# One normalisation for the nine softmax sums of a pair of heads, in the first batch

## The chip, the cores and the metric

The kernel runs on one core of one Trainium2 chip. The metric is the device time of one execution in microseconds, the median of several runs; lower is better. The core has a tensor engine for matrix products (PE, with its weight loads shown apart as PEld), a vector engine (DVE), a scalar engine (ACT), GpSimd (POOL), and a queue for transfers (SP). Each engine works through its own instructions in the order in which the program has them; engines wait for one another by semaphores.

## The reference

Three stages stand one behind the other; the change is in the first, in its first batch.

```python
# q, k, v: (4, 8, 576, 64); blocks of 64; a query sees its own block and those before it
scores = np.matmul(q, k.transpose(0, 1, 3, 2)) / np.sqrt(64)
scores = np.where(block_i >= block_j, scores, -1e9)
attn = np.exp(scores - np.max(scores, axis=-1, keepdims=True))
attn = attn / (np.sum(attn, axis=-1, keepdims=True) + 1e-09)
x = np.matmul(attn, v)                     # then laid out as 2304 tokens of 512
...
x = np.maximum(np.maximum(x @ w1, x @ w2), x @ w3) @ w_out          # 512 -> 768 -> 512
...
for e in range(4):                          # 512 -> 1024 -> 512 for each expert
    out += p[:, e:e + 1] * (np.maximum(x @ w1[e], 0.0) @ w2[e])
```

## The kernel before, in words

**The stages.** The attention is computed batch by batch, eight heads a batch, two heads (a pair) at a time. The first feed-forward stage (moe1, L549) of a batch is put between the attention of the next batch, in small steps. The experts come last and are the larger part of the time; they are almost nothing but matrix products. The weights of moe1 are converted during the first batches (class Convert, L417: two steps on ACT, L452 and L454, then POOL L459, DVE L461 and L462, POOL L466, ACT L85 and DVE L475).

**Scores of a head.** 576 queries are four blocks of 128 rows and one of 64. The last 64 rows of both heads of a pair share a fifth block, p4. scores(g, grp) (L163) computes head g in two groups: group 0 holds the blocks 0, 2 and 3, group 1 the block 1, and for the odd head of a pair the shared block as well. Each block is a product in PSUM (L190, L195), a row minimum on DVE (L208) and an exponential on ACT (L215), which also writes the row sum into one column of sm. So a pair has nine columns of sums: four for each head and one for the shared block.

**Normalising.** scores leaves a function normalise (L221) behind, which is called once the next step has been written (stage, L599). It adds 1e-9 to the sums of its group (DVE L223) and takes the reciprocal (DVE L224). In batches 1 to 3 POOL then multiplies each block by its reciprocals (L236). In batch 0 (g < H) only the shared block p4 is multiplied so. The other blocks stay as they are; POOL copies their reciprocals, each one 64 times side by side, into rb (L232), a part of the large tile arena that is free at that time. For each pair these are four copies, of 192 or of 64 elements a partition.

**Behind it.** turn_probs (L259) transposes the probabilities on PE (L274) into PSUM tiles tt, and DVE or ACT copies them to eh (L299; the shared block by L283). values32 (L311) multiplies them by v on PE (L320, L328, L332), and ACT copies the result to xf (L339 to L346). weigh (L349) transposes rb into a PSUM tile rt (L355), and DVE multiplies xf by it (L358). moe1_inputs (L537) splits xf into two parts (L546, L547).

**Buffers.** The score tiles of group 0, tt and rt all come from one pool of four PSUM banks, the x pool; the tile of the odd head's group 1, which holds the shared block, comes from a pool of one tile of its own, c. There are two tiles p4, one for each of two pairs in flight, and three tiles sm for the sums, one a head.

**What sets the order.** The loop over heads (L621) writes the steps of a head in the order of a list, todo; the code that it writes is then ordered for each engine by the framework's planner, on a timeline that it works out while the kernel is built (`schedule_with_timeline_sim=True`). So an engine's order in the trace is not always that of the source: work of the conversion stands between that of the heads, and the group of a head that has a buffer free can come ahead of its other group.

Of the kernel before, what the change touches and what calls it, by code (L numbers as in the profile page):

```python
# [18 lines left out]
P = 128  # L19
# [5 lines left out]
def program(tc, q, k, v, w123, w_out, probs, e_w1, e_w2, out):  # L25
    nc = tc.nc

    B, H, D, S = q.shape[0], 2 * q.shape[1], q.shape[2] // 2, q.shape[4]
# [5 lines left out]
    NPAIR = H // 2  # L34
# [22 lines left out]
    arena = big.tile([P, KD * NT], F32, name="arena")  # L57
# [24 lines left out]
    pairs, heads, later, made = {}, {}, [], {}  # L82
# [80 lines left out]
    def scores(g, grp):  # L163
        pair, h = pairs[g // 2], g % 2
        if grp == 0:
            heads[g] = dict(
                p=[None] * 4,
                mn=ap_.tile([P, 5], F32, name="mn", tag="mn", bufs=3),
                sm=ap_.tile([P, 5, 2], F32, name="sm", tag="sm", bufs=3),
            )  # L170
        mn, sm, pt = heads[g]["mn"], heads[g]["sm"][:, :, 0], heads[g]["p"]
        masked = g < 2 * H
        c0 = 3 * grp
        sets = []
        for tag, cols, plan in GROUPS[1][h] if grp else GROUPS[0]:
            st = (ps_x if tag == "x" else ps_c).tile([P, cols], F32, name="st", tag=tag)
            sets.append((st, plan))
            for i, o, w in plan:

                if i == 4:  # L180
                    todo = [(QT + 64 * x, x) for x in range(2)]
                else:
                    todo = [(h * QT // 2 + P * i, h)]
                c = 0
                while c < w:
                    n = min(w - c, 512 - (o + c) % 512)
                    terms = [(part, q0, x) for q0, x in todo for part in ("q1", "q2")]
                    ends = masked and i < 4 and c + n == w
                    for m, (part, q0, x) in enumerate(terms):
                        nc.tensor.matmul(  # L190
                            out=st[:, o + c:o + c + n], lhsT=pair[part][:, q0:q0 + P],
                            rhs=pair["kk"][:, x, c:c + n], start=m == 0, stop=m == len(terms) - 1 and not ends,
                        )
                    if ends:
                        nc.tensor.matmul(  # L195
                            out=st[:, o + w - 64:o + w], lhsT=corner, rhs=corner[:, 0:64], start=False, stop=True
                        )
                    c += n
        c = c0
        done = []  # L200
        for st, plan in sets:
            for i, o, w in plan:
                if i < 4 and not masked:
                    nc.vector.memset(st[lo, o + w - 64:o + w], 1e30)
            mine = [(c + n, *x) for n, x in enumerate(plan)]
            c += len(plan)
            for col, i, o, w in mine:
                nc.vector.tensor_reduce(mn[:, col:col + 1], st[:, o:o + w], axis=AX.X, op=ALU.min)  # L208
            for col, i, o, w in mine:
                x = ap_.tile([P, w], F32, name=f"p{i}", tag=f"p{i}", bufs=2 if i == 4 else 3)  # L210
                if i == 4:
                    pair["p4"] = x
                else:
                    pt[i] = x
                nc.scalar.activation(  # L215
                    x, st[:, o:o + w], ACTF.Exp, bias=mn[:, col:col + 1], scale=-1.0,
                    accum_out=sm[:, col:col + 1],
                )
                done.append((col, x))

        def normalise():  # L221
            cs = slice(c0, c)
            nc.vector.tensor_scalar(sm[:, cs], sm[:, cs], 1e-9, None, op0=ALU.add)  # L223
            nc.vector.reciprocal(sm[:, cs], sm[:, cs])  # L224
            if g < H:

                if grp == 0 and h == 0:
                    o = 4 * (g // 2) * P
                    pair["rb"] = arena[:, o:o + 4 * P].rearrange("p (i h c) -> p i h c", i=4, h=2)
                rb = pair["rb"][:, 0:3, h] if grp == 0 else pair["rb"][:, 3:4, h]  # L230
                rs = sm[:, c0:c] if grp == 0 else sm[:, c - 1:c]
                nc.gpsimd.tensor_copy(rb, rs.unsqueeze(2).to_broadcast([P, c - c0 if grp == 0 else 1, 64]))  # L232
            for col, x in done:
                if g < H and x is not pair.get("p4"):
                    continue
                nc.gpsimd.tensor_scalar(x, x, sm[:, col:col + 1], 1.0, op0=ALU.mult, op1=ALU.mult)  # L236

        later.append(normalise)


# [372 lines left out]
    all_of(prep_pair(0))  # L613
    load_pair(2)
    stage(scores, 0, 0)
    stage(scores, 0, 1)
    stage(all_of, prep_pair(1))
    load_pair(3)
    stage(scores, 1, 0)
    stage(scores, 1, 1)  # L620
    for g in range(NG_):  # L621
# [15 lines left out]
        for n, st in enumerate(todo):  # L637
# [8 lines left out]
            at = (g + (n + 1) / len(todo)) / H  # L646
# [552 lines left out]
    def tile_in(pool, tag, shape, dt, bufs=1):  # L1199
        if early.get((pool, tag)):  # L1200
            return early[pool, tag].pop(0)
        return pool.tile(shape, dt, name=tag, tag=tag, bufs=bufs)
# [69 lines left out]
    for p in range(1, NPASS):  # L1272
        es = list(range(E))[::-1] if p % 2 else list(range(E))
        background = mix() if p < NPASS - 1 else iter(())
        for m, e in enumerate(es):
# [4 lines left out]
            for n, i in enumerate(order):  # L1280
                if n % 2 == 0:
                    h = parts[f"hq0{n // 2}"] if m % 2 == 0 else tile_in(p3, f"hq1{n // 2}", HQ, F32)
# [85 lines left out]
```

## Time and profile before

| | |
|---|---|
| median of 3 runs | 1252.12 us (1251.15 to 1253.44) |
| profiled execution | 1249.5 us |
| its span, first to last instruction | 1247.6 us |
| PE busy in the span | 1210.9 us |
| DVE busy in the span | 934.0 us |
| mean granted clock of PE, as a share | 0.997 |

The span is that of one execution under the profiler; the 1.9 us between it and the execution's own time lie around it. Batch 0's attention ends at about 88 us of the span.

### The profile page before, as it was taken

The page shows a single profiled execution, that of the slowest core. Times are in us where ns is not written, and L with a number is a line of the kernel's source. Part 1 is how long each engine was busy: PE and PEld are TensorE (multiplying, and loading weights), DVE is VectorE, ACT ScalarE, POOL GpSimd, SP SyncE. Part 2 cuts the span into 40 slices and gives each one's busy share as a digit, 9 for nine tenths or more (in the row PEclk, how much of TensorE's full clock was granted, in tenths as well). Part 3 has the DMA queues.
Part 4 walks back from the last instruction along what each step waited for, and adds up shares of the span by engine and source line. Part 5 has one row for each costly group of instructions (what it writes and reads, how often), then busy time and mean ns, then how long its engine had stood idle before and what let it go on. Part 6 is the DMA issues. An engine that isn't in the chain of part 4 may idle for free.

```text
span 1247.6 us, 19748 instructions
## 1 busy us (share of the span) xinstructions
PE 1210.9 (97%) x7433; PEld 1157.6 (93%) x7433; DVE 934.0 (75%) x1720; ACT 516.4 (41%) x1076; POOL 339.0 (27%) x428
## 2 busy tenths in 40 slices
PE   6889998999999999999999999999999999999998
PEld 5668997999999999989999998999999999999998
DVE  8979888666565634378888886758787788586896
ACT  7976767544544421234434441233232222322232
POOL 3648786454344212243333341000000000000000
PEclk9999999999999999999999999999999999999999
DMA  8745475545533488479888865778787887766754
GB/s 320 266 144 194 162 263 167 168 151 156 182 103 118 120 298 293 154 305 336 306 308 297 312 239 169 281 279 317 294 310 308 313 315 289 253 251 235 253 203 178
DMA packets 82644, 299.69 MB, mean 240 GB/s; under 512 B 8748, under 2 KB 18036, under 8 KB 69492
## 3 DMA queue, kind: packets, MB, share of 16 engines
q1 hardware_dynamic: 82548, 298.42, 67.2%
q8 instruction: 59, 0.97, 0.3%
q14 instruction: 37, 0.30, 0.1%
HBM read 215.26 MB, written 83.14 MB: 239 GB/s over the span
## 4 chain that ended last, share of the span: by engine, by line
PE 71%; DVE 13%; DMA 7%; ACT 4%; issue 3%; POOL 2%; SPq 0%; DVEq 0%; ACTq 0%; POOLq 0%
PE m L883 22%; PE m L528 19%; PE o L1042 17%; DMA t<-in_e_w 3%; PE st L190 3%; PE pv L382 2%; PE tt L274 2%; PE m L1042 2%; DMA part<-in_e_w 2%; DVE mn L208 2%; PE o L965 1%; PE o L968 1%; PE o L969 1%; PE pv L328 1%; DVE w L838 1%
## 5 line engine op out<-in xcount | busy, mean ns | idle before, releaser
L528 PE MATMUL m<-xh,wt 128*128 128x288 f32 x1120 | 238.8, 298 | 1.9 <-DVE mt L566 1.6
L883 PE MATMUL m<-t,w 128*128 128x384 f32 x1152 | 228.5, 336 | 0.0
L1042 PE MATMUL o<-hx,w 128*128 128x384 f32 x1176 | 225.8, 337 | 0.0
L1042 PEld LDWEIGHTS o<-hx,w 128*128 128x128 f32 x1176 | 207.9, 188 | 0.0
L883 PEld LDWEIGHTS m<-t,w 128*128 128x128 f32 x1152 | 203.3, 188 | 2.6 <-DVE tmp L903 0.4
L528 PEld LDWEIGHTS m<-xh,wt 128*128 128x128 f32 x1120 | 183.8, 188 | 2.8 <-DVE mt L566 2.0
L883 PE MATMUL m<-b,w 128*128 128x384 f32 x864 | 175.7, 337 | 2.9 <-ACT tmp L908 2.9
L528 PE MATMUL m<-xl,wt 128*128 128x288 f32 x560 | 165.2, 295 | 0.0
L883 PEld LDWEIGHTS m<-b,w 128*128 128x128 f32 x864 | 153.2, 188 | 6.0 <-ACT tmp L908 3.2
L528 PEld LDWEIGHTS m<-xl,wt 128*128 128x128 f32 x560 | 105.2, 188 | 0.3
L903 DVE TENSOR_TENSOR tmp<-m,tmp 128x384 f32<-128x384 f32 x144 | 77.8, 549 | 18.7 <-PE m L883 18.3
L236 POOL TENSOR_SCALAR p<-p,sm 128x128 f32<-128x128 f32 (+4 forms) x112 | 73.7, 674 | 46.5 <-DVE sm L224 17.5
L528 PE MATMUL m<-hh,wo 128*128 128x288 f32 x384 | 81.3, 299 | 2.7 <-ACT arena L577 1.3
L215 ACT ACTIVATE p<-st,mn 128x128 f32<-128x128 f32 (+3 forms) x144 | 78.4, 554 | 8.3 <-DVE mn L208 7.8
L1013 ACT CAST hx<-hq 128x768 fp32r<-128x768 f32 x49 | 40.5, 836 | 99.2 <-PE o L1042 76.1
L190 PE MATMUL st<-kk,q 128*128 128x128 f32 (+4 forms) x336 | 70.3, 339 | 7.5 <-ACT q L133 5.3
L965 PE MATMUL o<-w,hh 128*128 128x512 f32 x192 | 74.7, 391 | 0.8 <-ACT hh L943 0.5
L968 PE MATMUL o<-w,hh 128*128 128x512 f32 x192 | 74.7, 390 | 0.0
L969 PE MATMUL o<-w,hl 128*128 128x512 f32 x192 | 74.1, 390 | 0.0
L838 POOL TENSOR_TENSOR w<-part,w 128x512 fp32r<-128x512 f32 x32 | 48.8, 1547 | 88.7 <-ACT w L836 71.3
L566 DVE TENSOR_TENSOR mt<-m,mt 128x288 f32<-128x288 f32 x96 | 43.1, 452 | 39.1 <-PE m L528 38.6
L208 DVE TENSOR_REDUCE mn<-st 128x1 f32<-128x128 f32 (+3 forms) x144 | 66.4, 504 | 2.8 <-PE st L195 2.5
(173 smaller groups left out, 2182.0 us busy)
## 6 DMA issues: line engine op xcount, KB each, us to landing
w<-kb SPq DMA_DIRECT2D x55, 1024.0 KB, 5.5
w<-ka SPq DMA_DIRECT2D x30, 1792.0 KB, 7.5
ka<-w SPq DMA_DIRECT2D x16, 1792.0 KB, 6.7
wt<-held SPq DMA_DIRECT2D x54, 512.0 KB, 4.1
kb<-part SPq DMA_DIRECT2D x16, 1024.0 KB, 6.9
kb<-w SPq DMA_DIRECT2D x16, 768.0 KB, 5.2
arena<-in_w SPq DMA_DIRECT2D x18, 512.0 KB, 4.1
wo<-held SPq DMA_DIRECT2D x12, 768.0 KB, 4.5
```

What stands on the lines that cost most here:

```text
L190: nc.tensor.matmul(out=st[:, o + c:o + c + n], lhsT=pair[part][:, q0:q0 + P], rhs=pair["kk"][:, x, c:c + n], start=m == 0, stop=m == len(t ...
L208: nc.vector.tensor_reduce(mn[:, col:col + 1], st[:, o:o + w], axis=AX.X, op=ALU.min)
L215: nc.scalar.activation(x, st[:, o:o + w], ACTF.Exp, bias=mn[:, col:col + 1], scale=-1.0, accum_out=sm[:, col:col + 1],)
L236: nc.gpsimd.tensor_scalar(x, x, sm[:, col:col + 1], 1.0, op0=ALU.mult, op1=ALU.mult)
L528: nc.tensor.matmul(out=out_, lhsT=w, rhs=x, start=m == 0, stop=m == n - 1)
L838: eng.tensor_tensor(w[:, a:b, 1], raw[:, a:b], f(w[:, a:b, 0]), op=ALU.subtract)
L883: ins = nc.tensor.matmul(out=m, lhsT=a, rhs=b, start=start and n == 0, stop=stop and n == 3 * KH - 1, skip_group_check=True,)
L903: nc.vector.tensor_tensor(t, x, y, op=ALU.add)
L965: ins = nc.tensor.matmul(out=o, lhsT=hh[:, ts], rhs=wh, start=i == 0, stop=False)
L968: nc.tensor.matmul(out=o, lhsT=hh[:, ts], rhs=wl, start=False, stop=False)
L969: nc.tensor.matmul(out=o, lhsT=hl[:, ts], rhs=wh, start=False, stop=i == G - 1)
L1042: nc.tensor.matmul(out=o, lhsT=a, rhs=b, start=start and m == 0, stop=stop and m == 2, skip_group_check=True,)
```

## The change

In batch 0 the sums of both heads of a pair stand in one strip of 18 columns of the arena (every second one is used), behind the region of rb. The exponentials write them there in the order of the blocks 0, 1, 2, 3 of the one head, those of the other, and the shared block. normalise does nothing in three of the four groups of a pair; in the last one (odd head, group 1) it adds 1e-9 to all nine sums, takes one reciprocal of nine, and has POOL copy eight of them into rb in one instruction of 512 elements a partition. The multiplication of p4 by the ninth follows. Batches 1 to 3 are as before.

```diff
+            if g < H:
+                o = 4 * NPAIR * P + 18 * (g // 2)
+                heads[g]["sm"] = arena[:, o:o + 18].rearrange("p (c two) -> p c two", two=2)
...
+                at = col if g >= H else 8 if i == 4 else 4 * h + (0, 3, 1, 2)[i]
                 nc.scalar.activation(
                     x, st[:, o:o + w], ACTF.Exp, bias=mn[:, col:col + 1], scale=-1.0,
-                    accum_out=sm[:, col:col + 1],
+                    accum_out=sm[:, at:at + 1],
                 )
-                done.append((col, x))
+                done.append((at, x))
 
         def normalise():
-            cs = slice(c0, c)
+            if g < H and not (grp and h):
+                return
+            cs = slice(0, 9) if g < H else slice(c0, c)
             nc.vector.tensor_scalar(sm[:, cs], sm[:, cs], 1e-9, None, op0=ALU.add)
             nc.vector.reciprocal(sm[:, cs], sm[:, cs])
             if g < H:
 
-                if grp == 0 and h == 0:
-                    o = 4 * (g // 2) * P
-                    pair["rb"] = arena[:, o:o + 4 * P].rearrange("p (i h c) -> p i h c", i=4, h=2)
-                rb = pair["rb"][:, 0:3, h] if grp == 0 else pair["rb"][:, 3:4, h]
-                rs = sm[:, c0:c] if grp == 0 else sm[:, c - 1:c]
-                nc.gpsimd.tensor_copy(rb, rs.unsqueeze(2).to_broadcast([P, c - c0 if grp == 0 else 1, 64]))
+                o = 4 * (g // 2) * P
+                pair["rb"] = arena[:, o:o + 4 * P].rearrange("p (i h c) -> p i h c", i=4, h=2)
+                nc.gpsimd.tensor_copy(
+                    pair["rb"].rearrange("p i h c -> p h i c"),
+                    sm[:, 0:8].rearrange("p (h i) -> p h i", h=2).unsqueeze(3).to_broadcast([P, 2, 4, 64]),
+                )
```

## Rows read from the trace of the kernel before

**Rows 1.** The page's first part: busy us of each engine.

```profile
PE 1210.9 (97%) x7433; PEld 1157.6 (93%) x7433; DVE 934.0 (75%) x1720; ACT 516.4 (41%) x1076; POOL 339.0 (27%) x428
```

**Rows 2.** Windows: stretch: us, busy PE, PEld, DVE, ACT, POOL, clock, DMA.

```profile
10.00:66.00 56.00, 46.62 (x271) 35.14 (x270) 52.88 (x107) 52.03 (x136) 31.38 (x44) 0.97 0.79 284
...
92.00:1248.00 1156.00, 1137.90 (x7020) 1101.95 (x7018) 856.22 (x1566) 441.69 (x882) 294.56 (x357) 1.00 0.67 240
```

**Rows 3.** Waits of PE from 10 to 92 us: total, times, longest.

```profile
PE pv L328 <- ACT eh L299: 4.8, 2, 2.5
PE tt L274 <- DVE eh L299: 2.3, 1, 2.3
...
PE tt L274 <- DVE xf L358: 1.3, 1, 1.3
```

**Rows 4.** The chain from 10 to 66 us: shares, then pieces (start, us).

```profile
by line: DVE mn L208 14.5%; PE pv L328 9.6%; issue 9.1%; DVE spare L135 6.9%; PE st L190 6.5%; DVE q L135 6.4%; DVE kk L122 6.1%; DVE eh L299 5.5%; DVE spare L122 5.2%; ACT spare L85 3.9%; DVE arena L461 3.8%; DVE sm L223 3.7%; DVE arena L4
...
15.54 0.14 DVE sm L224 x2
...
19.51 0.45 DVE sm L223
...
38.81 0.09 DVE sm L224
```

**Rows 5.** Instructions on tile sm, 10 to 67 us: ns min/median/max, forms.

```profile
L223 DVE TENSOR_SCALAR sm<-sm x16: 139/157/1179, 13.2 to 65.4; 128x3 f32<-128x3 f32 x8, 128x1 f32<-128x1 f32 x4, 128x2 f32<-128x2 f32 x4
L224 DVE RECIPROCAL sm<-sm x16: 131/164/178, 15.5 to 65.6; 128x3 f32<-128x3 f32 x8, 128x1 f32<-128x1 f32 x4, 128x2 f32<-128x2 f32 x4
L232 POOL COPY arena<-sm x16: 236/339/1180, 15.8 to 66.8; 128x192 f32<-128x192 f32 x8, 128x64 f32<-128x64 f32 x8
```

**Rows 6.** Timeline around 41 us and 65 us: start, us, engine, line.

```profile
40.70 1.26 POOL L466 TENSOR_TENSOR arena<-arena 128x512 int32<-128x512 int32 x1 [1.29 <-DVE arena L462]
40.81 1.18 DVE L223 TENSOR_SCALAR sm<-sm 128x3 f32<-128x3 f32 x1
...
41.91 0.68 DVE L358 TENSOR_TENSOR xf<-rt,xf 128x512 f32<-128x512 f32 x1
...
42.51 0.16 DVE L224 RECIPROCAL sm<-sm 128x3 f32<-128x3 f32 x1
42.59 0.65 DVE L299 COPY eh<-tt 128x512 f32<-128x512 f32 x1
...
65.41 0.15 DVE L223 TENSOR_SCALAR sm<-sm 128x3 f32<-128x3 f32 x1
...
65.60 0.18 DVE L224 RECIPROCAL sm<-sm 128x3 f32<-128x3 f32 x1
```

**Rows 7.** Timeline: p4 and its transposes in pairs 1, 2 and 3.

```profile
30.60 0.81 POOL L236 TENSOR_SCALAR p<-p,sm 128x576 f32<-128x576 f32 x1
...
33.70 0.21 ACT L215 ACTIVATION_READ_ACCUMULATOR p<-st,mn 128x1 f32 x1
...
36.16 0.63 PE L274 MATMUL tt<-ident,p 128*128 128x128 f32 x4 [0.40 <-ACT eh L299]
...
38.73 0.16 DVE L224 RECIPROCAL sm<-sm 128x3 f32<-128x3 f32 x1
...
46.36 2.96 PE L328 MATMUL pv<-eh,vraw 128*128 128x512 f32 x8
...
53.54 0.87 PE L274 MATMUL tt<-ident,p 128*128 128x128 f32 x6 [2.27 <-DVE eh L299]
...
55.25 0.17 DVE L224 RECIPROCAL sm<-sm 128x3 f32<-128x3 f32 x1
...
67.08 1.25 PE L274 MATMUL tt<-ident,p 128*128 128x128 f32 x10
```

**Rows 8.** POOL's groups by form, 10 to 67 us: busy us, mean ns.

```profile
L232 POOL COPY arena<-sm 128x192 f32<-128x192 f32 x8 | 4.2, 530 | 6.1 <-DVE sm L224 6.1
...
L232 POOL COPY arena<-sm 128x64 f32<-128x64 f32 x8 | 2.4, 294 | 2.5 <-DVE sm L224 1.7 <-DVE sm L223 0.5 <-ACT wo L85 0.2
```

## The prediction

> **What bounds the kernel now.** I read the page's head first [rows 1]: the tensor engine (PE) is busy for 1210.9 of 1247.6 us, so whatever shortens the run has to shorten the 36.7 us in which PE stands still. A table by stretch shows where these lie [rows 2]. From 92 us on PE works 1137.9 of 1156 us. In the stretch from 10 to 66 us, which is most of batch 0 and holds every instruction that the change touches, it works only 46.6 of 56 us, while the vector engine (DVE) works 52.9 and ScalarE 52.0. So batch 0 is bound by DVE and ScalarE together, and all the rest by PE. POOL has 24.6 us to spare there.
>
> The third view is what PE waited for between 10 and 92 us [rows 3]: copies of transposed probabilities by ScalarE (4.8 us) and by DVE (2.3 us), and 1.3 us for the multiplication in L358. These are engines that come late with a short operation because their queue is full. The chain of waits for the same stretch [rows 4] says which operations fill it: reductions L208 hold 14.5% of it, and L223, the tiny add that the change thins out, 3.7%, which is 2.07 us of 56. The reciprocals L224 stand on the chain five times; the first piece has 0.14 us, the last 0.09, and the five together 0.62.
>
> **What is removed.** Per pair of heads the sums get one add and one reciprocal in place of four each. In the stretch there are 16 of each now [rows 5], so 12 adds, 12 reciprocals and 12 of 16 broadcast copies go. None costs its data: an add takes 139 ns at its shortest and 157 at its median, a reciprocal 131 to 178, on one to three numbers a partition. What DVE loses is the time to the next start: a reciprocal holds the next instruction for 0.08 us where that doesn't depend on it (42.51 to 42.59), and an add for 0.19 where its reciprocal follows (65.41 to 65.60) [rows 6].
>
> One add is different, that of head 4's first group, which will have none of its own. It starts at 40.81, 0.11 us after a POOL L466 began, and takes 1.18 us in place of 0.16; it ends at 41.99, 0.03 us after L466 [rows 6]. Behind it stands L358, which starts at 41.91, and PE's transposes wait 1.3 us for L358 [rows 3]. On the chain this add has some 1.1 us; another has 0.45 [rows 4]. So of the 2.07 us of the adds some 1.4 are waits for POOL (1.1 and 0.45, less 0.08 for each as an add without a wait). The Trainium skill (SBUF — State Buffer, Who interferes with whom) says that a DVE tensor_scalar that can run two-ported takes a port pair that it shares with GpSimd, as an exclusive lock for the whole instruction. By that page the add's wait ends with L466, and the trace agrees (0.03 us apart).
>
> Off the chain of waits: 2.07 + 0.62 = 2.69 us. Four adds and four reciprocals stay, now of nine columns. From one column to three an add grows by no more than the 18 ns between minimum and median, so nine cost it some 0.05 us more at most. Back to back the two cost 0.19 + 0.08 = 0.27 us, four such pairs 1.1 us. This leaves -1.6 us. The bounds: if the four remaining pairs fall off the chain, -2.7; if they wait for POOL as long as the two adds did (1.4 us more), -0.2.
>
> The Trainium skill (Perfetto Trace Analysis, Optimizing Scalar/DVE Operations) gives DVE some 60 ns of data access per instruction on SBUF. As an estimate from that page, 24 instructions would be 1.4 us of DVE's queue, against the 1.6 us above.
>
> **POOL's copies.** Sixteen copies take 6.6 us now, eight of 192 elements and eight of 64 [rows 8]. Undisturbed the larger take 0.34 us (the median of all sixteen is the least of the larger), the smaller 0.24, the minimum [rows 5]. 128 elements more then cost 0.10 us, and 512 elements 0.24 + 3.5 x 0.10 = 0.60 us. By the means of the two forms, 530 and 294 ns, it is 0.294 + 3.5 x 0.236 = 1.12 us, the upper end. Four copies are 2.4 to 4.5 us, so POOL has 2.1 to 4.2 us less to do; I take 0.60 for one, since the means hold waits. I cost that at nothing, since POOL is idle for 24.6 of 56 us [rows 2]; if it became the bound it would be worth those microseconds.
>
> **What gets a new wait.** The ninth sum scales p4, the shared last block of both heads, on POOL (L236). Before, its add had to wait only for the odd head's second group of scores. Now it waits for all nine sums, that is also for the odd head's first group, and the larger copy stands ahead of it on POOL. In this trace that first group is done after the second. Pair 1 shows it [rows 7]: p4 is scaled at 30.60 to 31.41, but the last sum of the odd head's first group is written at 33.91, and its reciprocal stands at 38.73 on DVE. With that reciprocal (0.16), 0.60 us of copy and 0.81 of scaling, p4 is ready at 40.3. Its transposes on PE begin at 36.16 now, so they would be 4.1 us late. They take buffers in the x pool of PSUM, which are handed out, as far as I can follow the trace, in the order of the source; what comes behind in that pool (scores, rt) then waits for one of the other two. The result itself is needed only at 46.36, by the odd head's values.
>
> In pair 2 the same sum gives 55.25 + 0.17 + 0.60 + 0.81 = 56.8 against transposes from 53.54: 3.3 us late. In pair 3 it is 65.60 + 0.18 + 0.60 + 0.81 = 67.2 [rows 6] against 67.08, which is nothing [rows 7]; pair 0 I price like pair 3. But the late places of those reciprocals come from their low urgency: nothing waited for them. With p4 behind it, the reciprocal can stand right behind the sums; then p4 is ready at 33.91 + 0.27 + 0.60 + 0.81 = 35.6 in pair 1, ahead of 36.16. So this edit costs 0 at the lower end and 4.1 + 3.3 = 7.4 us at the upper. I take 0.2, near the lower end, because PE also has work of its own in pair 1 to put in between: two products of head 2 (L320 and L328, eight matmuls of the latter) stand right there. What stands behind the waiting add on DVE are the reductions of the next heads, for which ScalarE's exponentials wait; behind the waiting copy on POOL stand L459 and L466.
>
> The new place of the sums, columns of the arena behind rb, costs nothing: the arena's first batch is not written again before L577, the output of the first feed-forward stage. Left as they are: the exponentials with their accumulators, the four transposes of rb and L358.
>
> **Sum.** -1.6 + 0.2 = -1.4 us. The profiled execution took 1249.5 us with its span of 1247.6, which is 2.6 under the median of 1252.12; the change is set against the median: 1250.7 us.
>
> **The rivals.**
> 1. A larger gain. The order of the work is planned anew, and with a freer DVE queue the late copies of [rows 3] come earlier as well. If the 2.3 us behind DVE and half of the 4.8 us behind ScalarE vanish too, the run is 1.4 + 2.3 + 2.4 = 6.1 us shorter, 1246.0; with one of them 3 to 4, some 1248.5. For it: each stands behind a full queue. Against it: ScalarE is as full as DVE [rows 2] and has nothing taken away. Centre 1247.5.
> 2. The waits for POOL move on. The adds that stay, or a DVE copy behind them, meet the next L466 as the add at 40.81 did; then the 1.4 us come back and the time is 1252.1. Against it: fewer adds and fewer copies can meet. By the skill's rule quoted above every remaining tensor_scalar on DVE can still be locked out.
> 3. Slower. p4 comes late in pairs 1 and 2. It decides once p4 is ready later than the x pool needs its buffers again, about 39 us in pair 1, when the four transposes of rb and the next scores want theirs (rt has to be ready for the L358 at 41.91, and p4 is so at 40.3). Then at least the 1.6 us of the gain are lost, and at most all 7.4 us come on top of -1.6: 1252.1 to 1257.9, centre 1255.5. For it: the gap between the two groups is in the trace in pairs 1 and 2. Against it: ten microseconds lie between the transposes and their use.
>
> **How the numbers follow.** The likeliest case, -0.2 to -3.2 us, has 0.40; I give it 1250.7, in its own range of 1248.9 to 1251.9. Rival 1 has 0.22, rival 2 0.14, rival 3 0.24. What can be told from no change is 0.2%, 2.5 us. Faster than that: all of rival 1 and 0.11 of the likeliest, 0.33. Slower: rival 3 but for 0.01, 0.23. Within: 0.44. The range reaches into rival 1 down to 1246.5 and into rival 3 up to 1256.0, and leaves out about 0.08 at either end.
>
> **What the changed profile would show.** Right: four adds and four reciprocals of nine columns and four POOL copies of 512 elements near 0.6 us before 70 us; no add over 1 us ahead of an L358; PE's busy time between 10 and 66 us up by 1 to 2 us, and the tail from 92 us on as long as it was. Wrong: PE waits at L274 for p4 (POOL L236), or at L190 for a buffer behind such transposes, which is rival 3; an add or copy on DVE that ends with a POOL instruction in another place, which is rival 2. The forecast is wrong also if the new order moves work of batch 1 or of the weights' conversion so that PE waits more after 92 us; nothing in this trace prices that.

## The result and the profile after

The changed kernel takes 1258.51 us (median of 4 runs, 1258.09 to 1261.09) against 1251.98 for the kernel before on the same chip: 6.5 us slower, ratio 1.0055 (95% interval 1.0038 to 1.0073). I had forecast 1250.7 us, in a range from 1246.5 to 1256.0. The profiled execution took 1258.09 us with a span of 1256.3.

The head of its page and the windows answer to [rows 1, 2]. In the windows the columns are the stretch, its length, busy time of PE, its weight loads, DVE, ACT and POOL, PE's clock, the DMA share and GB/s.

```profile
PE 1216.2 (97%) x7433; PEld 1161.9 (92%) x7433; DVE 931.3 (74%) x1696; ACT 516.6 (41%) x1076; POOL 336.1 (27%) x416
```

```profile
10.00:66.00 56.00, 43.94 (x247) 33.10 (x247) 49.14 (x77) 49.08 (x130) 26.84 (x30) 0.94 0.78 284
66.00:92.00 26.00, 21.17 (x105) 14.45 (x105) 17.04 (x36) 17.97 (x50) 13.31 (x17) 0.87 0.40 127
92.00:1248.00 1156.00, 1142.55 (x7047) 1106.94 (x7046) 858.03 (x1571) 445.69 (x891) 294.68 (x357) 1.00 0.67 240
```

DVE has 24 instructions fewer and POOL 12, as intended. But between 10 and 66 us PE works 43.9 us where it worked 46.6: the first batch comes forward more slowly. I follow three marks through the traces: the first transpose of rb in the last pair (the end of batch 0's attention), the first matmul of the first feed-forward stage and the first matmul of the experts. Before they stand at 85.24, 88.1 and 518.45 us, after at 91.24, 94.1 and 524.63. The delay of 6.0 us at the first mark is 6.2 at the last one, so it arises in batch 0. From the last mark to the start of the last expert matmul 697.2 us pass in the profiled execution of before and 699.4 after; as it is 698.9 to 700.2 in the kernels of the experiments, those 2.2 us belong to that one execution of before.

The waits of PE from 10 to 92 us name a wait that [rows 3] don't have. Behind the arrow stands who was waited for, then total us, times and the longest.

```profile
PE tt L280 <- POOL p L242: 3.4, 2, 2.4
PE st L193 <- DVE eh L305: 3.3, 1, 3.3
PE pv L334 <- ACT eh L305: 3.3, 3, 1.3
PE pv L326 <- ACT eh L305: 2.5, 2, 1.7
```

The first row is p4: its transposes (tt, L280, L274 before) wait twice for its scaling on POOL (L242). The chain of waits from 33 to 46 us shows the longer of the two, in pair 1 (start, us, what).

```profile
33.59 2.88 PE pv L334 x8
...
36.71 2.65 DMA vraw<-in_v
39.37 0.07 issue
39.44 0.73 POOL vs L87
40.17 0.07 issue
40.24 1.76 POOL vs L153
42.00 1.02 POOL arena L235
43.02 1.17 POOL p L242
44.18 0.04 issue
44.23 0.67 PE tt L280 x4
```

The timeline has what happened on ACT and DVE meanwhile: the last of the pair's nine sums, the add of nine columns and its reciprocal.

```profile
35.11 0.20 ACT L219 ACTIVATION_READ_ACCUMULATOR p<-st,mn 128x1 f32 x1
```

```profile
34.76 2.50 DVE L135 SCALAR_TENSOR_TENSOR spare<-raw,spare 128x1024 fp32r<-128x1024 f32 x2
37.18 0.68 DVE L305 COPY eh<-tt 128x512 f32<-128x512 f32 x1
37.78 0.15 DVE L229 TENSOR_SCALAR arena<-arena 128x9 f32<-128x9 f32 x1
37.85 2.35 DVE L211 TENSOR_REDUCE mn<-st 128x1 f32<-128x128 f32 x5
40.11 0.21 DVE L230 RECIPROCAL arena<-arena 128x9 f32<-128x9 f32 x1
```

Read together: the last sum is there at 35.31 us. The add stands behind L135 and an eh copy until 37.78, the reciprocal behind five reductions of the next heads until 40.11. Then copy (L235) and scaling (L242) stand on POOL behind L87 and L153, and L87 waits for the load of a pair's v. p4 is ready at 44.19: 8.9 us from the last sum, where I had worked out 1.7 (0.27 + 0.60 + 0.81). Of the prices, those of undisturbed instructions held, as the answers to [rows 5] show (ns least, median, most): the copy of 512 elements, of which I said 0.60 us, takes 0.61 at its least, and 0.81 at the median.

```profile
L229 DVE TENSOR_SCALAR arena<-arena x4: 155/238/457, 18.9 to 71.2; 128x9 f32<-128x9 f32 x4
```

```profile
L230 DVE RECIPROCAL arena<-arena x4: 203/207/212, 19.8 to 71.4; 128x9 f32<-128x9 f32 x4
```

```profile
L235 POOL COPY arena<-arena x4: 610/810/1069, 20.1 to 71.7; 128x512 f32<-128x512 f32 x4
```

### The profile page after: what moved, and what is told of

It reads as the page before. It is cut to its first block, busy times and chain, and to the rows that moved or that the text cites. A ratio compares the mean times of both kernels' runs of the same rounds, so it can differ in the third digit from the quotient of the medians.

```text
span 1256.3 us, 19712 instructions
## 1 busy us (share of the span) xinstructions
PE 1216.2 (97%) x7433; PEld 1161.9 (92%) x7433; DVE 931.3 (74%) x1696; ACT 516.6 (41%) x1076; POOL 336.1 (27%) x416
## 4 chain that ended last, share of the span: by engine, by line
PE 73%; DVE 9%; DMA 7%; ACT 5%; POOL 3%; issue 2%; SPq 0%; ACTq 0%; DVEq 0%; POOLq 0%
PE m L889 22%; PE m L534 20%; PE o L1048 16%; PE st L193 4%; DMA t<-in_e_w 3%; PE tt L280 2%; PE pv L388 2%; DMA part<-in_e_w 2%; PE m L1048 2%; PE o L971 1%; PE o L974 1%; PE o L975 1%; ACT p L219 1%; DVE w L844 1%; PE pv L334 1%
## 5 line engine op out<-in xcount | busy, mean ns | idle before, releaser
L242 POOL TENSOR_SCALAR p<-p,sm 128x128 f32<-128x128 f32 (+4 forms) x108 | 70.5, 668 | 53.0 <-DVE sm L229 17.0
```

## The experiments

Theory A: the loss is p4's way through nine sums, one add, one reciprocal and a copy. Theory B, the rival: the order of the work was planned anew, and the loss is what the new order does elsewhere. Times are medians in us, ratios are to the kernel before in the same series, and "p4" is the sum of PE's waits for POOL's p4 up to 96 us.

**Is it the wait?** Two kernels that differ from before in as little as possible. Both write the nine sums into one strip and the reciprocals into a separate place; all sixteen adds, reciprocals and copies stay. In e2 the add and reciprocal of the group with p4 take all nine sums, in e3 their own two alone.

```diff
+                to = pair["inv"][:, grp and h, :, 0]
+                cs = slice(0, 9) if grp and h else ...   # e3: its own two columns
...
-            nc.vector.reciprocal(sm[:, cs], sm[:, cs])
+            nc.vector.reciprocal(to[:, cs], to[:, cs])
```

> As the kernel before, with its 16 adds, 16 reciprocals and 16 copies in batch 0, but the last add and reciprocal of a pair take in all nine raw sums, so that p4 waits as in the changed kernel; nothing is saved. Theory A: the loss without the saving, 1256 to 1261 us, with PE waiting 2 to 5 us at L274's transposes for POOL p. Theory B: nothing grew, 1250.5 to 1253.5 us.

> Control for the run with the wait alone: the same strip of sums and the same separate place of the reciprocals, but the last add and reciprocal of a pair take only the two sums of their own group, as before. Theory A and theory B both: 1250.5 to 1253.5 us; a time outside of it would be what a mere re-planning of the order is worth.

e2: 1259.24, ratio 1.0042 (1.0028 to 1.0056). e3: 1253.10, ratio 1.0001 (0.9992 to 1.0009). e2 takes 6.1 us more than e3, and its trace has about as much of waits for p4:

```profile
PE tt L285 <- POOL p L247: 5.8, 4, 2.6
```

So rival 3's mechanism is there with nothing merged, and the difference is about as large as the whole loss. But the order of each of the two was planned by itself, so this alone doesn't say how much of the 6.1 us is the wait. The strip and the separate place cost nothing that shows.

**Parts of p4's way.** In e1 p4 keeps an add and a reciprocal of its own and is scaled ahead of the copy; the other eight sums are merged.

```diff
+            if g < H:
+                nc.vector.tensor_scalar(sm[:, 8:9], sm[:, 8:9], 1e-9, None, op0=ALU.add)
+                nc.vector.reciprocal(sm[:, 8:9], sm[:, 8:9])
+                x = pair["p4"]
+                nc.gpsimd.tensor_scalar(x, x, sm[:, 8:9], 1.0, op0=ALU.mult, op1=ALU.mult)
+            cs = slice(0, 8) if g < H else slice(c0, c)
```

> As the changed kernel, but the ninth sum (p4's) gets an add and a reciprocal of its own and p4 is scaled before the other eight sums are touched; so p4 no longer waits for the odd head's first group, and the eight others still have one add, one reciprocal and one copy. Theory A (p4 waits for sums it does not need, and PE for p4): no wait of PE at L280 for POOL p in batch 0, the first transposes of rb back near 40 us from 45.1, and 1249.5 to 1252.5 us. Theory B (the new order brings DVE and POOL instructions into collision on large operations; the long copy is part of that): 1256 to 1260 us, as the changed kernel.

1254.57, ratio 1.0011 (1.0000 to 1.0021), p4 0. Most of the loss is gone, but the time lies between the ranges of the two theories. e4 is the changed kernel with p4 only scaled ahead of the copy:

```diff
             nc.vector.reciprocal(sm[:, cs], sm[:, cs])
             if g < H:
+                x = pair["p4"]
+                nc.gpsimd.tensor_scalar(x, x, sm[:, 8:9], 1.0, op0=ALU.mult, op1=ALU.mult)
```

> As the changed kernel, but on POOL p4 is scaled ahead of the copy of 512 elements; the wait for all nine sums stays. Theory A: p4 is ready earlier by the copy's 0.6 to 1.1 us in pairs 1 and 2, so 1256.0 to 1258.0 us. Theory B: no difference, 1257.5 to 1259.5 us.

1252.24, ratio 0.9997 (0.9986 to 1.0008), p4 0.3. That is 6.3 us less than the changed kernel in its own series (7.3 by the ratios), and less than either theory had it, while the copy holds p4 for no more than 1.1 us at a time. Its trace has the sums of pair 1 at about the same time, and everything behind them earlier:

```profile
35.29 0.17 DVE L229 TENSOR_SCALAR arena<-arena 128x9 f32<-128x9 f32 x1
35.37 1.74 DVE L211 TENSOR_REDUCE mn<-st 128x1 f32<-128x128 f32 x4
37.02 0.20 DVE L230 RECIPROCAL arena<-arena 128x9 f32<-128x9 f32 x1
```

```profile
37.44 0.74 POOL L236 TENSOR_SCALAR p<-p,arena 128x576 f32<-128x576 f32 x1
38.13 0.80 POOL L237 COPY arena<-arena 128x512 f32<-128x512 f32 x1
40.61 0.72 POOL L87 TENSOR_SCALAR vs<-vraw 128x640 fp32r<-128x640 f32 x1 [1.68 <-DMA vraw<-in_v]
```

Scaling and copy now stand ahead of L87, which waits for its load after them. A swap of two POOL instructions had the whole order planned anew. e5 and e6 leave p4's scaling out, of the changed kernel and of the kernel before; e7 gives the scaling to DVE (`nc.vector` in place of `nc.gpsimd`); e8 keeps L87 and L153 of later pairs behind p4's scaling (`tc.issue_after`); e9 traces the normalisation of a pair one step earlier.

> As the changed kernel, but p4 is not scaled in batch 0 (part left out: the last 64 rows of batch 0's heads are not divided by their sums), so nothing on the way to p4's transposes waits for the sums; one add, one reciprocal and one copy a pair stay. Theory A (the loss is the way through the sums to p4): 1249.5 to 1252.0 us. Theory B (re-planning and collisions of DVE and POOL): the 4 scalings of 0.75 us go from POOL, the rest stays, 1256 to 1259 us.

> The same in the kernel before (part left out: the same), with its four adds, reciprocals and copies a pair: the control for the run above. Theory A: the kernel before had slack there, so 1251 to 1253.5 us, and the changed kernel without the scaling is 1 to 2.5 us faster than this one, which is the merging's own worth. Theory B: as theory A for this kernel, and the changed kernel without the scaling slower than this one by 3 to 6 us.

> As the changed kernel, but p4 is scaled by DVE, right behind the reciprocal, and POOL only copies. Theory A: without POOL's queue (the copy of 0.6 to 1.1 us, and the vs work that stands ahead of it in pair 1) p4 is ready 2 to 3 us earlier in pair 1; DVE has four operations of some 0.5 us more: 1252.5 to 1256.0 us. Theory B: DVE has more to do and can still collide, 1257.5 to 1260.5 us.

> As the changed kernel, but POOL's two vs operations for pair 4 (2.5 us, which waited for their transfer) may not stand ahead of the scaling of p4 of pair 2, nor those of pair 5 ahead of that of pair 3. Theory A, if POOL's queue is the price: copy and scaling of pair 1 start at the reciprocal, some 1.6 us earlier, 1256.0 to 1257.5 us. If the late reciprocal alone is the price, or by theory B: 1257.5 to 1259.5 us.

> The changed kernel with nothing left out, but in batch 0 the add, reciprocal, copy and scaling of a pair are traced right behind the odd head's second group of scores, where the changed kernel traces them one step later. So the planner gives them their turn earlier. Theory A (the loss is the way of p4 through the nine sums): PE's waits for POOL's p4 in batch 0 fall from 7.8 us to under 2 us, and the time falls by 3 to 6 us against the changed kernel, to 1252.5 to 1255.5 us. Theory B (the loss is what the newly planned order does elsewhere, above all DVE and POOL in each other's way at 20 to 28 us and late copies): p4's waits may fall, and the time stays at 1256.5 to 1259 us.

| kernel | time | ratio (95%) | p4 |
|---|---|---|---|
| e5 after, p4 not scaled | 1253.91 | 1.0006 (0.9998 to 1.0015) | 0 |
| e6 before, p4 not scaled | 1255.00 | 1.0013 (1.0003 to 1.0023) | 0 |
| e7 p4 scaled by DVE | 1257.59 | 1.0042 (1.0029 to 1.0055) | 0 |
| e8 L87 and L153 behind p4 | 1258.31 | 1.0042 (1.0030 to 1.0054) | 1.3 |
| e9 traced one step earlier | 1260.23 | 1.0052 (1.0040 to 1.0065) | 3.9 |

e5 lies between the two ranges. e6 is a warning: work taken out, and the time rises, against both theories; what is left to explain it is the new order. e7 and e8 speak for B: the waits for p4 go or fall to 1.3 us (in e7 PE has no wait for DVE's p4 either), and the time stays. e8 fits A as well if the late reciprocal alone is the price, as its expectation allowed: in pair 1 it stands at 41.25 us. In e9 the edit didn't bring about what I expected of it: in pair 1 the reciprocal still stood behind five reductions. (The 7.8 us in its expectation are a slip: in the waits of the changed kernel shown above PE waits 3.4 us for p4.) As long as each edit has the order planned anew, A and B can't be told apart by such edits.

Two more of that kind trace e1 and e4 one step earlier, and e12 leaves the adds of 1e-9 out of the kernel before.

> As the kernel in which p4 has an add and a reciprocal of its own and is scaled ahead of the copy, the other eight sums having one add, one reciprocal and one copy; traced right behind the odd head's second group of scores besides. Nothing is left out. Theory A: no PE wait for p4 again, so what shows is the gain of 8 fewer adds and 8 fewer reciprocals, some 1 us: 1251 to 1254.5 us, no worse than where it was traced later (1254.57). Theory B: the order decides, and the time can lie anywhere between 1250 and 1258 us without a wait for p4.

> As the changed kernel with p4 scaled ahead of the copy of 512 elements, and traced right behind the odd head's second group of scores besides. Nothing is left out. If it is the way of p4 that decides (A), both edits shorten the same way and do not add up: 1250.5 to 1253.5 us, with under 0.5 us of PE waits for p4, about what p4 scaled first had alone (1252.24). If the order decides (B), it can differ from that run by 2 us or more in either direction while p4's waits are the same.

> The kernel before without the sixteen adds of 1e-9 in batch 0; it leaves that small number out and nothing else (reciprocals, copies and scaling are as before). It prices the part of the change that I costed as a gain. By the prediction the adds hold 2.07 us of the chain in batch 0, so A: 1250 to 1252 us, 1.5 to 2 us below the kernel before on the same chip, with batch 0 ending earlier by as much. B: the order is planned anew and gives the time back or more: 1252.5 to 1256 us, as the kernel before did when only its scaling of p4 was taken out (1255.0).

e10: 1255.50, ratio 1.0016 (1.0007 to 1.0025), p4 0.8. e11: 1253.29, ratio 1.0002 (0.9993 to 1.0011), p4 0. e12: 1251.79, ratio 0.9993 (0.9982 to 1.0003): sixteen adds are worth 1.0 us, with an interval of 2.3 gained to 0.4 lost. e11 and e12 lie in theory A's range, e10 is above it. None of them shows a gain over the kernel before that is clear of the noise.

**The order held.** The last six kernels name, at the end of the program, the place of the instructions in the queue of their engine, so that the order isn't planned anew:

```diff
+    for row in order:                       # one row for each engine
+        for a, b in zip(row, row[1:]):
+            tc.add_manual_dep(b, a.name, no_sync, reason="pin")
```

The order of e13, e14 and e15 is that of the kernel before. In e13 (merged as in e1) and e14 (merged as in the change) the merged add, reciprocal and copy stand where the last of the four stood. In e15 those of pairs 1 and 2 stand where the last sum is ready. e16 has the changed kernel's order.

> The order is held: every engine's instructions stand as in the kernel before, so nothing is planned anew. p4 keeps an add, a reciprocal and its scaling in their places; the other eight sums of a pair get one add, one reciprocal and one copy, in the place of the last ones. Nothing is left out. This prices the removal alone (8 adds, 8 reciprocals and 12 copies fewer). Theory A (what was removed has the worth that I gave it, and the wait for p4 is the loss): two thirds of the 1.6 us, up to 2 us: 1250.8 to 1252 us. Theory B (the order decides, the tiny instructions are worth nothing): 1252.5 to 1254 us, within 1 us of the kernel before.

> The changed kernel with the order held: every engine's instructions stand as in the kernel before, the merged add, reciprocal and copy in the place of the last of the four, and p4's scaling right behind that copy. Nothing is left out. This is the upper end of my step on p4: transposes 4.1 us late in pair 1 and 3.3 us in pair 2, with at most 1.6 us gained elsewhere. Theory A: PE waits for POOL's p4 6 to 8 us in all and the time is 1257 to 1260 us. Theory B (p4's lateness has room, and the loss of the changed kernel comes from the order planned anew): under 1255 us, though p4 is as late.

> As the changed kernel in the order of the kernel before, but in pairs 1 and 2 the merged add and reciprocal stand on the vector engine where the last of the nine sums is ready, ahead of L135 and L122, and copy and scaling on POOL ahead of the L465 that stands next; the order is otherwise held. Nothing is left out. This is the lower end of my step on p4, the reciprocal right behind the sums: p4 would be ready at about 36 us in pair 1 and 53 in pair 2. Theory A: PE's waits for p4 fall to under 1.5 us and the time is 1250.5 to 1253 us, 5 us or more under the late order. Theory B: the two orders differ by under 2 us.

> The changed kernel's order on every engine, held, except that on POOL the scaling of p4 and the copy of 512 elements change places in each of the four pairs. Nothing is left out. Scaled first and planned anew, this kernel took 1252.24 us, 6.3 us less than the changed one. p4 comes 1.07 us earlier in pair 1 and 0.61 in pair 2. Theory A (p4's lateness, wherever the order puts its reciprocal): the two waits fall by that, from 3.4 us to about 1.7, so 1256 to 1257 us; the other 4 us of that gain came with the order. Theory C (a late p4 costs more than the wait that the profile puts down to it): 1252 to 1255 us. Theory D (only the order counts): 1257.5 to 1259 us.

| kernel | time | ratio (95%) | p4 | last rb |
|---|---|---|---|---|
| e13 p4 with its own sum | 1252.04 | 0.9997 (0.9988 to 1.0006) | 0 | 88.59 |
| e14 nine sums, late | 1260.64 | 1.0070 (1.0057 to 1.0082) | 10.6 | 94.31 |
| e15 nine sums, early | 1254.63 | 1.0015 (1.0005 to 1.0025) | 3.1 | 87.99 |
| e16 after's order | 1259.41 | 1.0055 (1.0042 to 1.0067) | 4.1 | 90.38 |

("last rb" is the first mark of above; e13's profiled execution took 1256.24 us, the longest of its eleven, and the table's time is the median.) With the order held, the nine sums on p4's way cost 8.6 us at the late place (1260.64 less 1252.04) and 2.6 at the early one. e14 and e15 are even the same program: only the places of add, reciprocal, copy and scaling differ, in two pairs, and that is worth 6.0 us of time and 7.5 of waits for p4 (first e14, then e15):

```profile
PE tt L280 <- POOL p L242: 10.6, 3, 6.1
```

```profile
PE tt L280 <- POOL p L242: 3.1, 2, 2.2
```

At the late place theory A holds and goes past its own range (6 to 8 us of waits, up to 1260 us). At the early one A had the difference to the late place right (5 us or more), but the waits (3.1 us, not under 1.5) and the time (1253 at most) too low; e18 below leaves open whether p4 is all that is left there. e13 lies between the two ranges that I gave, and other waits stand in its trace where e14 waits for p4 (3.8 us of PE's scores for an eh copy of DVE, 0.4 in e14), so waits and time can't agree to the microsecond. In e16 the copy still stood ahead of the scaling, other than I had meant, so it is the changed kernel once more with its order named; it took as long as that one (ratio 1.0055 both), so naming the order costs nothing that shows.

e17 is what e16 should have been, and e18 is e15 with p4 scaled ahead of the copy.

> What the run scalefirst_order was meant to be (there the copy still stood ahead of the scaling, so it repeated the changed kernel): the changed kernel's order held on every engine, only that in the four pairs POOL scales p4 ahead of the copy of 512 elements. Nothing is left out. In the changed kernel p4 waits for the copy for 1.07 us in pair 1 and 0.61 in pair 2. Theory A (what p4 comes earlier is won, no more): the waits for p4 fall by 1.6 to 2 us from 3.4 to 4.1, and the time to 1256.5 to 1257.8 us. Theory C (planned anew, the same swap brought 6.3 us because a late p4 holds more behind it than its wait shows): 1252 to 1255.5 us. Theory D (only the order counts): 1258 to 1259.5 us.

> Both edits in the order of the kernel before: merged add and reciprocal where the last sum is ready (as early_order) and p4 scaled ahead of the copy on POOL. Nothing is left out. In early_order p4 still waited 2.2 us in pair 1 and 0.9 in pair 3 and the time was 1254.63 us. Theory A: p4 comes earlier by the copy, 1.4 us in pair 1 and 0.6 in pair 3, its waits fall under 1.2 us, and the time to 1252.3 to 1253.4 us, the level of own_order (1252.04) and of the kernel before. Theory D (only the order counts): it stays within 0.8 us of early_order.

e17: 1258.89, ratio 1.0057 (1.0042 to 1.0073), p4 2.5. e18: 1254.37, ratio 1.0010 (0.9999 to 1.0020), p4 0.3. Both went as theory D had it: the waits for p4 fall by 1.6 and 2.8 us, the ratio of e17 is no lower than that of e16, and that of e18 by 0.0005 (0.6 us) lower than that of e15. In e18 another wait took their place, of PE's scores for an eh copy of DVE (4.6 us at 30.00, 0.4 in e15); an L135 of 2.48 us beside POOL's L474 stands ahead of it, as at the end for e13. So no cost of the copy ahead of the scaling shows, though one of under 2 us could hide in the intervals. By e14 and e15 the cost is in the place of add, reciprocal and POOL's two instructions in the queues, and most of e4's gain came with its new order, not with the swap. What e15 still loses against e13 (2.6 us) can be p4 or such other waits.

None of the kernels beats the kernel before: the best that leave nothing out, e13 and e4, equal it.

## Why the prediction was wrong

**What bounds the kernel.** Right: all that happened lies in batch 0. Between the second mark and the third pass 430.4 us before and 430.5 after.

**What is removed, -1.6 us.** Not refuted, too small to be seen. e13 keeps the order and takes away 8 adds, 8 reciprocals and 12 copies: two thirds of 1.6 would be 1.1 us, measured are 0.6 less, with an interval from 1.5 less to 0.8 more.

**POOL's copies, 0; the strip, 0.** Right for the strip (e3), and no cost of the one long copy shows (e17). That taking twelve copies away changes nothing else was not right: without the copy at 24.79 us POOL's next instruction meets a long one of DVE in the changed kernel, as shown under the second cause.

**What gets a new wait, 0.2 us.** This is the step that failed, in the sentence that "the reciprocal can stand right behind the sums" because p4 now makes it urgent, so that I took a value near the lower of the bounds 0 and 7.4. Its place was right (pairs 1 and 2), and so was the row that showed it [rows 7]; the value was far too low: PE waits 3.4 us for p4 in the changed kernel, and 10.6 with the old order held (e14). Four things stood between the last sum and p4 in pair 1: other work of DVE ahead of the add (2.5 us), five reductions ahead of the reciprocal (2.3), L87 with a late load and L153 ahead of the copy (1.7 from the end of the reciprocal), and copy and scaling (2.2, with 1.07 and 1.17 in place of 0.60 and 0.81). That it can be otherwise e15 shows, with add and reciprocal named to their places:

```profile
35.43 0.68 DVE L229 TENSOR_SCALAR arena<-arena 128x9 f32<-128x9 f32 x1 [0.19 <-ACT p L219]
36.14 0.21 DVE L230 RECIPROCAL arena<-arena 128x9 f32<-128x9 f32 x1
```

```profile
36.49 1.42 POOL L235 COPY arena<-arena 128x512 f32<-128x512 f32 x1 [0.41 <-DVE arena L230]
37.99 0.74 POOL L242 TENSOR_SCALAR p<-p,arena 128x576 f32<-128x576 f32 x1
```

p4 is ready at 38.73 there, 3.3 us after its last sum, and even so its transposes wait 2.2 us. The add itself takes 0.68 us and ends at 36.11, 0.03 us after POOL's L472 (34.79 to 36.08), and the one in pair 2 takes 1.53: the waits for POOL that rival 2 had moving on are there too.

**The upper bound, 7.4 us,** was worked out for just the order of e14, and e14 went past it: 10.6 us of waits, 6.14 in pair 1 (4.1 worked out), 3.62 in pair 2 (3.3) and 0.89 in pair 3 (0). In pair 1 the scaling took 1.69 us beside DVE's L481 and L468 in place of 0.81, and the reciprocal stood 1.0 us later.

**"Ten microseconds lie between the transposes and their use"** was the argument against rival 3. It counts the use of the data. But PE takes its matmuls in order, and in e14 the values of the pair before (L326, L334), the next scores and the transposes of rb all stand behind p4's transposes. What counts is the next instruction in the queue, not the next reader.

**A second cause in the changed kernel.** Its delay begins before its first wait for p4. Counted in matmuls, PE is level with the kernel before at 25 us (90 done by 24.90 after, by 25.20 before). Ahead of the first wait for p4 it is 3.2 us behind: 151 are done by 38.40 us before and by 41.60 after (the number behind the first busy time).

```profile
0.00:38.40 38.40, 27.41 (x151) 21.11 (x152) 32.47 (x66) 31.48 (x80) 16.95 (x34) 1.00 0.86 310
```

```profile
0.00:41.60 41.60, 29.40 (x151) 22.09 (x151) 34.54 (x57) 32.13 (x83) 14.28 (x27) 0.96 0.80 293
```

In between PE's scores wait 3.34 us for an eh copy of DVE, 1.68 in the kernel before. That copy stands behind an L135 of 2.49 us, which runs beside POOL's L472; before, it took 1.54, and POOL's L466 started at 25.94, behind the copy L232 (24.79, 1.18 us), one of those that the change takes away. First the kernel before, then the changed one:

```profile
24.57 1.54 DVE L135 SCALAR_TENSOR_TENSOR q<-arena,q 128x1024 fp32r<-128x1024 f32 x2
27.10 0.44 PE L190 MATMUL st<-spare 128*128 128x128 f32 x2 [1.68 <-DVE eh L299]
```

```profile
24.88 2.49 DVE L135 SCALAR_TENSOR_TENSOR q<-arena,q 128x1024 fp32r<-128x1024 f32 x2
24.90 2.32 POOL L472 TENSOR_TENSOR arena<-arena 128x512 int32<-128x512 int32 x1 [1.27 <-DVE kk L122]
28.36 0.47 PE L193 MATMUL st<-spare 128*128 128x128 f32 x2 [3.34 <-DVE eh L305]
```

So rival 2's mechanism, a DVE instruction that meets a POOL instruction in another place, is in the trace together with rival 3's, at an instruction that neither rival named.

**What stays open.** In the changed kernel's own trace PE waits 3.4 us for p4, and the marks are 6.0 late. How much of the 6.0 is p4's, how much the meeting's and how much the lower clock after both (below) isn't settled. e7 and e8 lost all or most of the waits for p4 and not the time, and e17 lost 1.6 us of them and not the time. In e13 the meeting is in the trace too, and its median is that of the kernel before. Why e7's order is as slow I can't say. Shown with the order held is only what p4's place costs in the order of the kernel before.

## What to carry to other kernels

A merge makes every consumer wait for the last of its producers: before merging, look for the one consumer whose result is read by an engine in order (here p4, by PE), and leave that one out. Price the delay along the queues that the value has to pass, with what stands in them at that time, not by the durations of the instructions on its way; and where a planner orders the work, take the value at the place that the old order gives, not at the place that would be best. An instruction that looks free to remove can keep two others apart. To tell a cost from a new order, hold the order.

## What I had not expected of the hardware

A pause of PE can cost more than its length. In e14 PE stands still from about 36 to 42.4 us, and the windows show its clock behind that (0.50 is the lower level, 1.2 GHz):

```profile
36.00:40.00 4.00, 0.26 (x3) 0.02 (x1) 4.00 (x10) 3.41 (x11) 3.60 (x4) 0.76 0.64 199
40.00:44.00 4.00, 1.60 (x8) 1.60 (x9) 1.81 (x3) 0.45 (x1) 3.58 (x3) 0.50 0.90 336
44.00:48.00 4.00, 4.00 (x10) 2.61 (x10) 0.00 (x0) 2.39 (x8) 0.61 (x1) 0.50 0.63 214
```

Eight matmuls of L334 that follow take 4.05 us; in e13, at a clock of 1.00, the same eight take 2.11:

```profile
43.95 4.05 PE L334 MATMUL pv<-eh,vraw 128*128 128x384 f32 x8
```

```profile
40.56 2.11 PE L339 MATMUL pv<-eh,vraw 128*128 128x384 f32 x8
```

That is 1.9 us on top of a wait of 6.1. In the changed kernel the clock is 0.58 between 28 and 32 us, behind the scores' wait of 3.34, and 0.71 between 44 and 48, behind p4's of 2.38; before, it is 1.00 in both.

```profile
28.00:32.00 4.00, 3.65 (x16) 2.82 (x16) 2.74 (x6) 4.00 (x10) 0.84 (x3) 0.58 0.83 271
44.00:48.00 4.00, 3.50 (x22) 3.00 (x23) 2.35 (x4) 3.08 (x9) 2.74 (x4) 0.71 0.95 329
```

DVE and POOL can slow each other. L135 in two pieces takes 1.42 us in e15 with POOL idle, and 2.49 in e13, where POOL's L477 (L472 there) begins 0.23 us after it and takes 2.11 in place of 1.27:

```profile
25.50 2.49 DVE L135 SCALAR_TENSOR_TENSOR q<-arena,q 128x1024 fp32r<-128x1024 f32 x2
```

```profile
25.73 2.11 POOL L477 TENSOR_TENSOR arena<-arena 128x512 int32<-128x512 int32 x1 [1.16 <-DVE arena L473]
```

```profile
25.41 1.42 DVE L135 SCALAR_TENSOR_TENSOR q<-arena,q 128x1024 fp32r<-128x1024 f32 x2
```

```profile
27.32 1.27 POOL L472 TENSOR_TENSOR arena<-arena 128x512 int32<-128x512 int32 x1 [2.39 <-ACT arena L460]
```

The eh copy behind L135 then comes late, and PE's scores wait 3.8 us for it in e13 and 0.4 in e15. By the Trainium skill (SBUF — State Buffer, Who interferes with whom) a DVE instruction with two SBUF inputs contends with a GpSimd instruction that reads SBUF. The trace agrees: each of the two is longer by about 0.8 to 1.1 us. Whether the two meet hangs, as I read the traces, on when each becomes ready: but for what e13 takes away, the order on the queues is the same in e13 and in the kernel before, and there POOL's copy L232, one of those taken away, still stood in between. No run tests this by itself, and each trace is one execution, e13's the longest of its eleven.
